# Windowed attention with global tokens, then a routed feed-forward: keys kept in natural order, seven packed blocks of exponentials, AV moved in the turn, loads by pairs

## The chip, the cores and the metric

The kernel runs on one core of a Trainium2 chip. A core has five engines that run side by side, each from its own queue and in that queue's order: TensorE (PE; its weight loads are listed as PEld), VectorE (DVE), ScalarE (ACT), GpSimd (POOL) and SyncE (SP, which here only issues transfers). Sixteen DMA engines move data for all of them. An engine waits for another, or for a transfer, on a semaphore. The metric is the device time of one execution in microseconds (us), lower is better.

## The reference

Eight batches of eight heads. Each batch has 512 local tokens and 32 global tokens, with 64 channels a head. A local query sees the local keys at most 32 places away and all 32 global keys; a global query sees all 544 keys. The result, 4352 rows of 512, goes through eight experts, weighted by a Sinkhorn-normalised gate.

```
k_all = np.concatenate([k_g, k_l], axis=2); v_all = np.concatenate([v_g, v_l], axis=2)
out_g = np.matmul(sm(scale * np.matmul(q_g, k_all.transpose(0, 1, 3, 2))), v_all)
mask = np.abs(pos[:, None] - pos[None, :]) <= window          # window = 32
s_ll = np.where(mask, scale * np.matmul(q_l, k_l.transpose(0, 1, 3, 2)), -1000000000.0)
a_l = sm(np.concatenate([scale * np.matmul(q_l, k_g.transpose(0, 1, 3, 2)), s_ll], axis=-1))
out_l = np.matmul(a_l, np.concatenate([v_g, v_l], axis=2))
...
P = np.exp(x @ w_gate - max)      # then 8 rounds: rows to 1, columns to N / E
for e in range(E): out += P[:, e:e+1] * (np.maximum(x @ w1[e], 0.0) @ w2[e])
```

## The kernel before

Two phases follow each other. The order of every engine's instructions is the order in which the program writes them: `tc.manual_schedule()` keeps a scheduler out, and only semaphore waits are put in.

**Attention.** The unit is a pair of heads (32 pairs: `b, hp = divmod(p, HP)`, four pairs a batch). The main loop at L442 runs 35 turns, and a turn `i` works on several pairs at once, each in another stage:

- `stage_ak(i)`, `stage_aq(i)`: four 128x128 transposes on TensorE each, and copies out of PSUM. Rows lie in memory so that token 4p+s of a group is in partition p; the transposes give columns in the order (s, p) within a block of 128 tokens. The key copy (DVE, L303) keeps that order in `kTw`, a window for every query block `j`: 128 own keys, 32 global keys, 32 left and 32 right neighbours, 224 columns. GpSimd fills the last three parts (L304, L308, L309). The query copy (ACT, L319, twice) writes the two heads into two tiles `qTz` whose other half of partitions is zero.
- `stage_b(i-1, head, jp)`: scores of two query blocks, one 224-wide matmul each (L333), then on DVE a fused mask, scale and row minimum (L337). `stage_e` follows: the exponentials on ACT (L347) into `u`, a tile of four blocks of 256 columns; after the fourth block SP issues a DMA transpose of `u` into `uT`, eight 128x128 blocks (L351). So a pair has four `stage_b`, four `stage_e`, two DMA transposes.
- `stage_c(i-2)`, at the end of a turn: AV. For each head and block two matmuls of 65 columns: `uT` block 2j with the block's own values `va` (L363), block 2j+1 with `vb`, which holds the globals and both edges (L364). The 65th column is the row sum; DVE divides (L367, L370). PSUM holds one such result (`ps_o`, one buffer), shared with the global scores.
- `stage_d(i-3)`: TensorE transposes the result, DVE copies it into `xT` (L379).
- Every second turn (even `i`), `global_scores` (two 512-wide and two 32-wide matmuls, L386 and L390; the maximum on DVE, L394; the exponentials on ACT, L398) and later `global_norm` (GpSimd, L405). The turn after (odd `i`) holds `global_turn` (five transposes, L411) and `global_out` (twenty small matmuls, L426).
- After a batch's fourth `stage_d`: `gate` (L436), and the first expert's work for that batch goes into `queue`. `fill(1)`, eight times a turn, takes one piece from it: two 512-wide matmuls of layer 1 (L95; a relu on ACT after every second piece, L102) or layer 2 (L115; a copy on DVE after every fourth piece, L123).

Transfers: GpSimd's queue loads queries and keys for two pairs at a time every second turn (L187, 256 KB each as stored), and the next batch's values in four parts, two in each of two turns (L194). GpSimd also brings queries and keys into fp16 rows by block (L191). SP's queue issues the transposes and builds `vb` from `va` and `vg`: four transfers of globals, four of left and four of right edges a batch (L202, L208, L214). The first expert's weights are loaded whole at the end of turn 3 (`w1`) and turn 5 (`w2`).

**Experts.** After the loop (L549 on) the routing's Sinkhorn rounds run on DVE beside expert work, then experts 1 to 7 stream through TensorE.

Of the kernel before, what the change touches and what calls it, by code (L numbers as in the profile page):

```python
# [17 lines left out]
P = 128  # L18
# [4 lines left out]
def kernel(  # L23
# [28 lines left out]
    KW = P + Sg + 2 * WIN  # L52
# [95 lines left out]
    with ExitStack() as actx:  # L148
# [10 lines left out]
        Q4 = P // NJ  # L159
        NU, NK, NQ, VW = 4, 3, 2, Dh + 2  # L160
        mask = acst.tile([P, 3, KW], BF16)
# [3 lines left out]
        va_buf = [acst.tile([P, H, NJ, VW], FP16, name=f"va{i}") for i in range(2)]  # L165
        vb_buf = [acst.tile([P, H, NJ, VW], FP16, name=f"vb{i}") for i in range(2)]
        kTw_buf = [acst.tile([P, NJ, KW], FP16, name=f"kTw{i}") for i in range(NK)]
        qTz_buf = [acst.tile([P, Sl], FP16, name=f"qTz{i}") for i in range(2 * NQ)]
        u_buf = [acst.tile([P, NJ, 256], FP16, name=f"u{i}") for i in range(NU)]
        ug_buf = [acst.tile([P, 640], FP16, name=f"ug{i}") for i in range(2)]  # L170

        qk = {}

        raws = {}

        def new_qk(k):
            qk[k] = tuple(ain.tile([P, NJ, 4, Dh], FP16, tag=t, bufs=1, name=f"{t}_{k}") for t in ("q16", "k16"))
            return qk[k]

        def src_of(x, k):  # L180
            b, half = divmod(k, 2)
            return x[b, 4 * half : 4 * half + 4].rearrange("h (p s) d -> p h (s d)", s=NJ)

        def load_qk(k):
            raws[k] = tuple(ain.tile([P, 4, NJ * Dh], FP16, tag=t, bufs=1, name=f"{t}_{k}") for t in ("qr", "kr"))
            for dst, x in zip(raws[k], (q_l, k_l)):
                nc.gpsimd.dma_start(out=dst, in_=src_of(x, k))  # L187

        def order_qk(k):
            for dst, src in reversed(list(zip(new_qk(k), raws.pop(k)))):  # L190
                nc.gpsimd.tensor_copy(out=dst, in_=src.rearrange("p h (s d) -> p s h d", s=NJ))  # L191

        def load_va(b, s):
            nc.gpsimd.dma_start(out=va_buf[b % 2][Q4 * s : Q4 * (s + 1), :, :, 0:Dh].rearrange("p h j d -> p (h j) d"),  # L194
                                in_=v_l[b].rearrange("h (j p s) d -> s p (h j) d", p=Q4, s=NJ)[s])

        W8 = WIN // NJ

        def load_vb_left(b):
            va, vb = va_buf[b % 2], vb_buf[b % 2]  # L200
            for s in range(NJ):
                nc.sync.dma_start(out=vb[Sg + W8 * s : Sg + W8 * (s + 1), :, 1:NJ],  # L202
                                  in_=va[Q4 * (s + 1) - W8 : Q4 * (s + 1), :, 0 : NJ - 1])

        def load_vb_right(b):
            va, vb = va_buf[b % 2], vb_buf[b % 2]
            for s in range(NJ):
                nc.sync.dma_start(out=vb[Sg + WIN + W8 * s : Sg + WIN + W8 * (s + 1), :, 0 : NJ - 1],  # L208
                                  in_=va[Q4 * s : Q4 * s + W8, :, 1:NJ])

        def load_vb_globals(b, js):
            r0 = Sg * (b % 4)
            for j in js:
                nc.sync.dma_start(out=vb_buf[b % 2][0:Sg, :, j], in_=vg[r0 : r0 + Sg, b // 4])  # L214
# [9 lines left out]
        nc.sync.dma_start(out=sk, in_=src_of(k_l, 0))  # L224
        nc.scalar.dma_start(out=sq, in_=src_of(q_l, 0))
# [7 lines left out]
        mnat = out_nat[:, 26, :].bitcast(BF16)[:, 0 : 3 * KW].rearrange("p (v c) -> p v c", v=3)  # L233
        nc.gpsimd.memset(mnat[:, 0], 0.0)
# [6 lines left out]
        for x in range(NJ):  # L241
            load_va(0, x)

        for t_ in kTw_buf:
            nc.vector.memset(t_[:, 0, P + Sg : P + Sg + WIN], 0.0)
            nc.vector.memset(t_[:, NJ - 1, P + Sg + WIN : KW], 0.0)
# [5 lines left out]
        for t_ in u_buf:  # L252
            nc.vector.memset(t_[:, :, KW:256], 0.0)
# [388 lines left out]
```

## Time and profile before

| what | value |
|---|---|
| median of 3 runs | 1142.42 us (1139.2 to 1145.99) |
| the profiled execution | 1136.88 us, its span 1135.1 us, mean granted clock 0.985 |
| TensorE matmul busy | 1055.6 us (93%) |
| VectorE, ScalarE, GpSimd busy | 555.2, 348.3, 198.9 us |
| windows: 0 to 284 us | the attention's 35 turns; TensorE busy 10.5 us of the first 28, then between 15 and 26 us of each 28 or 29 |
| window 312 to 900 us | TensorE busy 588 us of 588 |

The profile's first lines cut the span into 40 slices of 28.4 us. Up to about 284 us TensorE has gaps; from about 312 us to the last slice it has none. Time can be taken from or added to the second part only by changing its matmuls, and the change does not touch them. So the whole question lies in the first 284 us, and every microsecond by which the attention ends sooner or later moves the end by as much.

### The profile page before, as it was taken

The page shows a single profiled execution, that of the slowest core. Times are in us where ns is not written, and L with a number is a line of the kernel's source. Part 1 is how long each engine was busy: PE and PEld are TensorE (multiplying, and loading weights), DVE is VectorE, ACT ScalarE, POOL GpSimd, SP SyncE. Part 2 cuts the span into 40 slices and gives each one's busy share as a digit, 9 for nine tenths or more (in the row PEclk, how much of TensorE's full clock was granted, in tenths as well). Part 3 has the DMA queues.
Part 4 walks back from the last instruction along what each step waited for, and adds up shares of the span by engine and source line. Part 5 has one row for each costly group of instructions (what it writes and reads, how often), then busy time and mean ns, then how long its engine had stood idle before and what let it go on. Part 6 is the DMA issues. An engine that isn't in the chain of part 4 may idle for free.

```text
span 1135.1 us, 16317 instructions
## 1 busy us (share of the span) xinstructions
PE 1055.6 (93%) x6266; PEld 532.8 (47%) x6266; DVE 555.2 (49%) x1361; ACT 348.3 (31%) x708; POOL 198.9 (18%) x274
## 2 busy tenths in 40 slices
PE   3587888779999999999999999999999999999997
PEld 2454555445444454445444444445444544454444
DVE  5566778667734444444444444444444444444443
ACT  5476777565531111111111121111111111121111
POOL 7454555442089000000000000000000000000000
PEclk9789999999999999999999999999999999999999
DMA  9999999993300413000400040004000400002222
GB/s 150 156 153 131 143 125 132 121 122 72 60 1 4 72 18 57 1 1 1 75 1 1 1 74 1 1 1 75 1 1 1 74 1 1 1 1 75 75 75 91
DMA packets 155550, 60.83 MB, mean 54 GB/s; under 512 B 122320, under 2 KB 147024, under 8 KB 155472
## 3 DMA queue, kind: packets, MB, share of 16 engines
q0 software_dynamic: 64368, 29.11, 21.6%
q1 hardware_dynamic: 90576, 30.15, 15.5%
q8 instruction: 49, 0.80, 0.3%
q10 hardware_dynamic: 528, 0.52, 0.1%
q14 instruction: 29, 0.24, 0.1%
HBM read 60.31 MB, written 8.91 MB: 61 GB/s over the span
## 4 chain that ended last, share of the span: by engine, by line
PE 80%; DMA 13%; DVE 3%; ACT 2%; issue 1%; SPq 1%; POOL 0%; DVEq 0%; ACTq 0%; POOLq 0%
PE ph L95 38%; PE py L115 38%; DMA uT<-u 11%; ACT u L347 1%; DMA va<-in_v_l_dram 1%; PE s L333 1%; DVE st L337 1%; ACT qTz L319 1%; DVE gm L394 1%; DMA out_nat<-in_v_g_dram 1%; PE po L363 1%; PE sa L386 0%; PE po L364 0%; SPq L202 0%; DMA mask<-out_nat 0%
## 5 line engine op out<-in xcount | busy, mean ns | idle before, releaser
L95 PE MATMUL ph<-xT,w1e 128*128 128x512 f16 (+1 forms) x2304 | 499.9, 368 | 0.3 <-DVE P_nat L438 0.3
L115 PE MATMUL py<-w2e,ht 128*128 128x512 f16 x2176 | 498.2, 380 | 0.0
L102 ACT ACTIVATE ht<-ph 128x512 f16<-128x512 f32 (+1 forms) x336 | 192.4, 573 | 683.7 <-PE ph L95 682.9
L95 PEld LDWEIGHTS <-w1e 128*128 128x128 f16 x2304 | 223.1, 98 | 220.7 <-issue 0.9
L115 PEld LDWEIGHTS <-ht 128*128 128x128 f16 x2176 | 211.0, 98 | 232.4 <-ACT ht L102 0.5
L125 DVE SCALAR_TENSOR_TENSOR out_nat<-py,P_nat,out_nat 128x512 f32<-128x512 f32 x238 | 178.7, 751 | 248.2 <-PE py L115 247.2
L104 DVE TENSOR_SCALAR ht<-ph 128x512 f16<-128x512 f32 (+1 forms) x240 | 158.4, 660 | 226.5 <-PE ph L95 224.7
L347 ACT ACTIVATE u<-st,nm 128x224 f16<-128x224 f32 x256 | 106.1, 472 | 49.6 <-DVE nm L337 43.5
L72 POOL DMA_DIRECT2D w1e<-in_moe_w_dram x7 | 5.4, 766 | 510.9 <-PE ph L95 506.0
L337 DVE CUSTOM_DVE_ANT_0 st<-s,mask 128x224 f32<-128x224 f32 x256 | 85.7, 385 | 7.7 <-ACT u L347 2.5
L333 PE MATMUL s<-kTw,qTz 128*128 128x224 f16 x256 | 49.7, 285 | 21.1 <-DVE nm L337 16.5
L363 PE MATMUL po<-va,uT 128*128 128x65 f16 x256 | 23.8, 200 | 35.8 <-DMA uT<-u 35.7
L600 POOL TENSOR_SCALAR out_nat<-out_nat,P_nat 128x512 f32<-128x512 f32 x32 | 49.6, 1561 | 35.7 <-DVE P_nat L597 35.7
L333 PEld LDWEIGHTS <-qTz 128*128 128x128 f16 x256 | 24.0, 105 | 45.3 <-issue 29.3
L319 ACT COPY qTz<-pq 64x512 f16<-64x512 f16 x64 | 36.9, 576 | 14.0 <-PE pq L316 13.2
L363 PEld LDWEIGHTS <-uT 128*128 128x128 f16 x256 | 19.4, 101 | 41.9 <-DMA uT<-u 38.7
L367 DVE RECIPROCAL rc<-po 128x8 f32<-128x8 f32 x32 | 6.6, 206 | 51.0 <-PE po L364 51.0
L405 POOL TENSOR_SCALAR ug<-ug,gr 128x544 f16<-128x544 f16 x16 | 26.2, 1638 | 17.5 <-DVE gr L404 17.5
L194 POOL DMA_DIRECT2D va<-in_v_l_dram x32 | 25.1, 792 | 2.8 <-PE s L333 2.2
L191 POOL COPY k<-kr 128x1024 f16<-128x1024 f16 x15 | 15.6, 1040 | 51.8 <-DMA kr<-in_k_l_dram 47.8
L364 PE MATMUL po<-vb,uT 128*128 128x65 f16 x256 | 23.8, 199 | 0.0
L370 DVE TENSOR_TENSOR xn<-po,rc 128x512 f16<-128x512 f32 x32 | 22.1, 691 | 1.1
(103 smaller groups left out, 424.8 us busy)
## 6 DMA issues: line engine op xcount, KB each, us to landing
w1e<-in_moe_w_dram POOLq DMA_DIRECT2D x8, 1024.0 KB, 8.1
w2e<-in_moe_w_dram POOLq DMA_DIRECT2D x8, 1024.0 KB, 10.3
out_dram<-out_nat SPq DMA_DIRECT2D x32, 256.0 KB
va<-in_v_l_dram POOLq DMA_DIRECT2D x32, 128.0 KB, 5.2
qr<-in_q_l_dram POOLq DMA_DIRECT2D x15, 256.0 KB, 5.2
kr<-in_k_l_dram POOLq DMA_DIRECT2D x15, 256.0 KB, 6.7
vb<-va SPq DMA_DIRECT2D x64, 24.8 KB
vb<-vg SPq DMA_DIRECT2D x32, 33.0 KB
```

The source lines that it names most:

```text
L95: nc.tensor.matmul(ph[:, 0:N], w1e[:, dk, P * fm : P * (fm + 1)], xT[:, dk, P * t0 : P * t0 + N], start=(dk == 0), stop=(dk == DP - 1))
L102: nc.scalar.activation(out=ht[:, 0:N], in_=ph[:, 0:N], func=AF.Relu)
L104: nc.vector.tensor_scalar(out=ht[:, 0:N], in0=ph[:, 0:N], scalar1=0.0, scalar2=None, op0=ALU.max)
L115: nc.tensor.matmul(py, hT[fk][:, P * c : P * (c + 1)], w2e[:, fk, :], start=(fk == 0), stop=(fk == FT - 1))
L125: nc.vector.scalar_tensor_tensor(out=out_nat[:, t, :], in0=py, scalar=P_nat[:, t, e : e + 1], in1=out_nat[:, t, :], op0=ALU.mult, op1=ALU.add)
L319: nc.scalar.copy(out=qTz_buf[2 * (p % NQ) + hi][r].rearrange("d (j s p) -> d j s p", j=NJ, s=NJ), in_=pt[r].rearrange("d s (j p) -> d j s ...
L333: nc.tensor.matmul(ps[:, jj, 0:KW], qTz[:, P * j : P * (j + 1)], kTw[:, j, :], start=True, stop=True)
L337: nc.vector.tensor_tensor_reduce(out=st[:, jj, :], in0=ps[:, jj, 0:KW], in1=mask[:, mvar[j], :], scale=-scale, scalar=3.0e38, op0=ALU.add, ...
L347: nc.scalar.activation(out=u[:, j, 0:KW], in_=st[:, jj, :], func=AF.Exp, scale=-1.0, bias=nm[:, jj : jj + 1])
L363: nc.tensor.matmul(o, uT[:, 2 * j, :], va[:, 2 * hp + hi, j, 0:W], start=True, stop=False)
L405: nc.gpsimd.tensor_scalar(out=ug[:, 0:S], in0=ug[:, 0:S], scalar1=rs, scalar2=None, op0=ALU.mult)
L600: eng.tensor_scalar(out=out_nat[:, t, :], in0=out_nat[:, t, :], scalar1=P_nat[:, t, 0:1], scalar2=None, op0=ALU.mult)
```

## The change

What is computed stays the same. In its parts:

1. **Keys in natural order.** `kTw` becomes `kT` (512 columns a pair): the DVE copy now writes tokens in order, so each element goes four places behind the one before it. The neighbours of a block are simply the columns beside it, so the three GpSimd copies go. A block's scores are now two matmuls: own keys with neighbours (192 wide, 160 at the two ends) and globals (32 wide, straight from `kgT`).
2. **Seven blocks.** The four widths 192, 224, 224, 192 are packed, with 32-column gaps, into 896 columns: seven 128x128 blocks to a DMA transpose. A transposed block can now hold parts of two query blocks, so AV takes 2, 3, 3 and 2 matmuls, ten a head instead of eight. `vo` holds seven sets of values that belong to the columns of shared blocks.
3. **Value edges.** Edges and globals land in `vo` in the partitions that they already have in `va`: five transfers a batch instead of twelve, each partition's bytes in one piece. `va` changes its layout to [block, head], loaded block by block.
4. **Queries.** One ACT copy into `qT`, then two GpSimd copies into the two `qTz`.
5. **AV** of a pair moves from the end of turn p+2 to turn p+3, after the second `fill`; `stage_d` of the same pair stays in turn p+3, now two fills from the end. Five buffers of `uT` instead of four.
6. **Order in the turn.** `global_scores` moves from after the third fill to after the fifth, just before `stage_aq`; `global_norm` goes behind both `order` copies; `gate` goes to the end.
7. **Loads.** Queries and keys by pairs, three turns ahead, each turn, at two places; values one block at a time in turns 4b-2 and 4b-1 and two in turn 4b for batch b; `w1` and `w2` in halves at the ends of turns 3, 4, 5 and 6.

```diff
-        kTw_buf = [acst.tile([P, NJ, KW], FP16, name=f"kTw{i}") for i in range(NK)]
+        U7 = 7 * P
+        OFF, WID = (0, 224, 480, 704), (192, 224, 224, 192)
+        AV = ((("a", 0, 0), ("o", 0, 1)), (("o", 3, 1), ("a", 1, 2), ("o", 1, 3)),
+              (("o", 4, 3), ("a", 2, 4), ("o", 2, 5)), (("o", 5, 5), ("a", 3, 6)))
+        kT_buf = [acst.tile([P, Sl], FP16, name=f"kT{i}") for i in range(NK)]
+        qT_buf = [acst.tile([P, Sl], FP16, name=f"qT{i}") for i in range(2)]
+        u_buf = [acst.tile([P, U7], FP16, name=f"u{i}") for i in range(NU)]
...
+        def order(t, p):
+            if p < B * HP:
+                rows[t, p] = ain.tile([P, NJ, 2, Dh], FP16, tag=t, bufs=2, name=f"{t}_{p}")
+                nc.gpsimd.tensor_copy(out=rows[t, p], in_=raw.pop((t, p)).rearrange("p h (s d) -> p s h d", s=NJ))
...
+        def load_vo_globals(b, part):
+            vo, src = vo_buf[b % 2], vg[Sg * (b % 4) : Sg * (b % 4 + 1), b // 4]
+            if part == 0:
+                nc.sync.dma_start(out=vo[32:64, 0:3], in_=src.unsqueeze(1).broadcast_to([Sg, 3, H, VW]))
+            else:
+                nc.sync.dma_start(out=vo[64:96, 5], in_=src)
+                nc.sync.dma_start(out=vo[0:32, 6], in_=src)
+        def load_vo_edges(b):
+            va, vo = va_buf[b % 2], vo_buf[b % 2]
+            nc.sync.dma_start(out=vo[96:128, 3:6], in_=va[96:128, 0:3])
+            nc.sync.dma_start(out=vo[0:32, 0:3], in_=va[0:32, 1:4])
...
         def stage_ak(p):
+            pt = turned("k", p)
+            nc.vector.tensor_copy(out=kT_buf[p % NK].rearrange("d (j p s) -> d j s p", j=NJ, s=NJ),
+                                  in_=pt.rearrange("d s (j p) -> d j s p", j=NJ))
         def stage_aq(p):
+            pt = turned("q", p)
+            qT = qT_buf[p % 2]
+            nc.scalar.copy(out=qT.rearrange("d (j s p) -> d j s p", j=NJ, s=NJ),
+                           in_=pt.rearrange("d s (j p) -> d j s p", j=NJ))
             for hi in range(2):
                 r = slice(Dh * hi, Dh * (hi + 1))
-                nc.scalar.copy(out=qTz_buf[2 * (p % NQ) + hi][r].rearrange("d (j s p) -> d j s p", j=NJ, s=NJ),
-                               in_=pt[r].rearrange("d s (j p) -> d j s p", j=NJ))
+                nc.gpsimd.tensor_copy(out=qTz_buf[2 * (p % NQ) + hi][r], in_=qT[r])
...
-                nc.tensor.matmul(ps[:, jj, 0:KW], qTz[:, P * j : P * (j + 1)], kTw[:, j, :], start=True, stop=True)
+                nc.tensor.matmul(ps[:, jj, w0 : w0 + k1 - k0], lhsT, kT[:, k0:k1], start=True, stop=True)
+                nc.tensor.matmul(ps[:, jj, g0 : g0 + Sg], lhsT, kg, start=True, stop=True)
```

The body of a turn after the change (`Bs`, `C` and `A` only say whether the turn has that pair; the once-only work of turns 0, 1, 9, 10, 12, 16 and 17 is left out):

```
stage_b(i-1, 0, 0);  fill(1)
stage_b(i-1, 0, 1);  stage_e(i-1, 0, 0);  fill(1)
stage_c(i-3);  stage_b(i-1, 1, 0);  stage_e(i-1, 0, 1);  load_pair("q", i+3);  fill(1)
stage_ak(i);  fill(1)
global_turn (odd i);  stage_b(i-1, 1, 1);  stage_e(i-1, 1, 0);  load_pair("k", i+3);  fill(1)
global_scores (even i);  fill(1)
stage_aq(i);  order("k", i+1);  stage_e(i-1, 1, 1);  load_va;  fill(1)
stage_d(i-3);  order("q", i+1);  global_norm (even i);  fill(1)
global_out (odd i);  gate, every fourth turn;  load_vo;  a half of w1 or w2 in turns 3 to 6
```

## The prediction

> **What bounds the kernel now.** I read the 40 slices first, to see where TensorE has gaps, then the waits of TensorE inside the gaps, then the chain of waits, then two turns of the timeline.
>
> ```profile
> PE   3587888779999999999999999999999999999997
> ...
> DMA  9999999993300413000400040004000400002222
> ```
>
> TensorE has gaps only in the first ten slices, and there the DMA engines are at nine tenths. Who ends TensorE's gaps between 20 and 260 us (total, times, longest):
>
> ```profile
> PE po L363 <- DMA uT<-u: 35.7, 19, 4.9
> PE s L333 <- DVE nm L337: 12.2, 21, 1.6
> ```
>
> The AV matmuls wait 35.7 us for transposed exponentials; the scores wait 12.2 us for VectorE. The chain between 100 and 200 us shows how long the transposes take (start, us):
>
> ```profile
> 130.67 6.94 DMA uT<-u
> ...
> 146.10 7.80 DMA uT<-u
> ...
> 162.82 13.21 DMA uT<-u x2
> ```
>
> One alone took 3.35 us (at 23.32, nothing else loading). The packets say why: of the transpose issued at 162.82 none starts before 165.5, since 256 KB loads of queries and keys, issued at 162.42 and 163.24, go through the same engines. This is delay by bursts, not a full DMA: between 161 and 163.5 no packet moves.
>
> A turn starts with its first score matmul. From the timeline: turn 1 at 11.0, 3 at 27.3, 8 at 73.3, 24 at 201.1, 28 at 234.9, 32 at 267.4. So turns 8 to 23 cost 127.8/16 = 8.0 us. Even turns that don't wait for a transpose take 6.67 (turn 12), with a gate 7.2; odd turns wait and take 7.8 to 10.5.
>
> The order behind the global scores matters after the change (start, us):
>
> ```profile
> 156.63 0.59 PE L386 MATMUL sa<-kTw,qgP 128*128 128x512 f16 x2
> ...
> 157.30 0.72 DVE L394 TENSOR_REDUCE gm<-sa 128x1 f32<-128x544 f32 x1
> ...
> 158.33 0.71 ACT L398 ACTIVATE ug<-sa,gn 128x544 f16<-128x544 f32 x1 [0.57 <-DVE gn L396]
> ...
> 160.75 1.17 ACT L319 COPY qTz<-pq 64x512 f16<-64x512 f16 x2
> 160.82 1.64 POOL L405 TENSOR_SCALAR ug<-ug,gr 128x544 f16<-128x544 f16 x1 [0.81 <-DVE gr L404]
> ...
> 165.35 0.44 PE L411 MATMUL pg<-identity,ug 128*128 128x128 f16 x5
> ```
>
> Today the normalisation (L405) ends 3 us before `global_turn` needs it, and the query copies come 1.7 us after `ug`. Both margins shrink below.
>
> **The change part by part.**
>
> *Transposes and AV.* Seven blocks for eight, fewer packets for `vo`, loads in halves: each lowers the delay; AV gets two fills, two score groups and itself more slack. The last transpose of a pair is issued at the end of `stage_e`, about 8.8 us into an even turn (below); its AV comes two turn starts later plus 1.4 us, some 9 us on. The worst transpose above took 15.03/2 = 7.5 us. So I cost the 35.7 us wait as gone; what is late next is worked out now. TensorE gets more matmuls: four 65-wide AV a turn at 0.031 us (161.14 to 161.62 for 16) and eight 32-wide scores at about 0.03 (gate: 16 in 0.54): 0.36 us a turn, and it is hidden wherever the chain below sets the turn.
>
> *The even turn, walked.* TensorE pieces: score group 0.25, fill 0.43, AV 0.62, four transposes 0.22, global scores 0.49. `global_scores` ends after four score groups, five fills, AV, key transposes and itself: 1.0 + 2.15 + 0.62 + 0.22 + 0.49 = 4.5. VectorE, in order: four reductions of score groups (0.31 each) to 1.9, reciprocal and division 0.22 + 0.69 from 2.2 to 3.1, reductions to 3.8, key copy 0.42 to 4.2, reductions to 4.9, maximum 0.73 and scaling 0.16 to 5.85. ACT: `ug` 0.71 + 0.19 to 6.8. Then in layer-1 turns a relu (0.59) comes first on ACT, in layer-2 turns an output copy (0.69) came first on VectorE; either way the query copy (0.58) ends at 8.0. Its GpSimd copy is a new operation, 64x512. Rows: 128 columns 0.306 (L304), 1024 columns 1.041 (L191). These are its bounds; the line between them gives 0.62, or 0.56 from one to the next, and I take that, since both rows are fp16 copies on that engine.
>
> ```profile
> L191 POOL COPY q<-qr 128x1024 f16<-128x1024 f16 x15 | 15.6, 1041 | 0.0
> ...
> L304 POOL COPY kTw<-kgT 128x128 f16<-128x128 f16 x32 | 9.8, 306 | 0.7 <-DVE kgT L279 0.7
> ```
>
> The next turn's first scores can start at 8.0 + 0.05 + 0.6 = 8.65. TensorE alone would have been there at 6.2 (6.8 with a gate).
>
> *The odd turn, walked.* On GpSimd behind the query copy stand the second one, two row orders, the value issues and the normalisation: 4 x 0.56 + 0.79 (one value load, L194) or 1.57 (two) + 1.6. From 8.05 that is 12.7 or 13.5, which is 4.05 or 4.85 into the odd turn, where `global_turn` stands at 3.3. After it come 0.27 + 0.25 + five transposes and fills (4 x 0.43 + 0.44) + `global_out` 0.5 = 3.2. Odd turn: 7.25 or 8.05.
>
> Two pairs of turns: 2 x 8.65 + 7.25 + 8.05 = 32.6, against 4 x 8.0 = 32.0 now. Five such groups, turns 8 to 27: +3 us. Turns 28 to 31: 16.7 + 8.65 + 6.6 = 32.0 against 32.5: nothing.
>
> *Key copy.* A strided write of the same 512 elements from the same PSUM tile is not in the trace; the bounds are 0.417 (L303) and 0.691 (L370, as many elements in fp32), and I take the nearest in input and type:
>
> ```profile
> L303 DVE COPY kTw<-pk 128x512 f16<-128x512 f16 x32 | 13.3, 417 | 1.5 <-PE pk L301 1.3
> ```
>
> At the upper bound each even turn's maximum is 0.27 later: 13 turns, +3.5 us, kept for the range. The Trainium skill, "VectorE: DVE Perf Modes", section "Mode 2×_1P — pack two bf16 into one 32-bit read", asks for a step of ±1 for two results a clock; by it this copy falls to one, and the estimate 512/0.96 GHz plus the 0.15 us that today's row leaves over is 0.68 us, so the sum would be 3.5 us worse.
>
> *Early turns.* Up to turn 7 there is no expert work, and weights load (151 GB/s from 11 to 64.6). Turns 3 to 7 cost 73.3 - 27.3 = 46.0, with transposes of 7.75, 10.55 and 15.03 us (two) on the chain. Walked as above without fills an even turn is VectorE's 5.3 (0.55 to the first reduction, eight of 0.31, 0.91, 0.42, 0.89) + `ug` 0.9 + 0.58 + 0.6 = 7.4, and an odd one between 6.4 and 8.0 by the value loads: about 37. That is -9. The lower bound of the gain is 2 us, if the same bytes at the same rate decide; weights in four pieces, 20 us earlier to 10 us later than now, speak against it, and I take -9. Turns 1 and 2 (mask and first loads) I leave: 17.9 and 27.1 by the same walk against 17.3 and 27.3.
>
> *Covered.* Seven SP issues fewer a batch (0.65 us each) leave SP, which waits 98.8 us for ACT's exponentials anyway. The three neighbour copies (0.85 us a turn) leave GpSimd, and two query copies (1.12) and one load issue (0.79, every turn of four) enter it; they matter only where counted. ACT saves 0.58 a turn, which is in the walk. If the covers of GpSimd go, its price is counted in rival two.
>
> *Sum:* 3 - 9 = -6 us on the profiled execution's 1136.9: 1131. It lies 5.5 us under the median, so on the median 1142.4 - 6 = 1136.4; I say 1136.
>
> **The rivals.**
>
> *One, TensorE becomes the bound.* If GpSimd's copies cost no more than the 0.306 row, the pair of turns shortens by 4 x 0.26 = 1.0 us, ten pairs -10: 1126. For: its row of 128 columns; 274 instructions and 18% busy. Against: L191 grows with the columns.
>
> *Two, slower: GpSimd's queue decides.* If each of those copies costs the 1.04 row, each pair of turns grows by 0.43 for the first scores' wait, and by 4 x 0.43 + 0.2 in all at `global_turn`, 1.9: ten pairs +19, 1155. The point from which the kernel is slower than before is 6/10 us a pair, a copy of about 0.7 us. For: L405 moved to the end of that queue and its reader did not move; a wait at either place stops all of TensorE. A VectorE copy at 0.69 adds to it. Against: the columns are half of that row's.
>
> *Three, the change doesn't take the wait away.* If DMA engines are in truth full, the transposes come later still and AV waits as now; turns stay at 8.0 and only the early 2 us are gained: 1140. For: nine tenths in nine slices. Against: the empty 2.5 us at 161, and the even turns of 6.67.
>
> **How the numbers follow.** Forecast 0.42, rival one 0.22, rival two 0.26, rival three 0.10. A measurement of this kernel can tell about 0.5% (5.7 us) from no change: below 1136.7 is faster, above 1148.1 slower. The forecast lies on the edge, with 3 us either way and 3.5 for the key copy: 0.23 faster, 0.15 same, 0.04 slower. One is faster. Two: 0.24 slower, 0.02 same. Three: 0.03, 0.05, 0.02. Sum: faster 0.48, same 0.22, slower 0.30. The forecast's own range is 1131 to 1143; to hold 8 in 10 it reaches to rival one with the early gain a little larger (1122) and to most of rival two (1153).
>
> **What would show it.** Right: in TensorE's waits "po from uT" falls below 5 us; "s from POOL qTz" appears in even turns with some 1.5 us each, and "pg from POOL ug" in odd turns; even turns last longer than odd ones; turn 8 starts near 64. Wrong: even turns near 7 us with no wait for `qTz` (rival one), GpSimd copies of 64x512 over 0.7 us (two), or `po` still waiting for `uT` (three). A GpSimd row, then, is what would upset the forecast most.

## The result, and the profile after

| kernel | median us | ratio to before, 95% interval | span of the profile | mean clock |
|---|---|---|---|---|
| before | 1142.1 (13 runs beside the changed kernel) | 1 | 1135.1 | 0.985 |
| after | 1147.95 (13 runs) | 1.0051 [1.0031, 1.0071] | 1144.1 | 0.981 |
| forecast | 1136 | 0.9944 | | |

The change costs half a per cent, 5.8 us; the forecast was a gain of 6. The slices of the changed kernel's page show where: TensorE still has gaps in the first ten slices and none behind, as before, the DMA engines are no fuller, and the granted clock of TensorE (PEclk) is below nine tenths in four of the first ten slices, where it was in two. PEclk before the change, then the slices after it:

```profile
PEclk9789999999999999999999999999999999999999
```

```profile
PE   2577978888999999999999999999999999999998
...
PEclk9889899989999999999999999999999999999999
DMA  9998999983400404000400040004000400002222
```

The waits of TensorE between 20 and 260 us (total, times, longest, us) are other ones. The wait of AV for `uT`, 35.7 us before, is not in the list any more. Two waits for GpSimd stand in its place, both named in the prediction:

```profile
PE s L320 <- POOL qTz L304: 28.9, 16, 3.0
PE pg L399 <- POOL ug L393: 10.8, 11, 2.6
```

Turns, by their first score matmul: turn 1 starts at 13.2, 3 at 30.7, 8 at 70.6, 24 at 207.4, 32 at 274.8. Turns 8 to 23 cost 136.8/16 = 8.55 us, against 8.0 before. Even turns take 8.73 or 8.83 (turn 10 took 9.49), odd ones mostly between 7.8 and 8.8; four in a row (12 to 15) sum to 34.05. Here is the chain of the even turn 14, which starts at 122.32 (start, us):

```profile
125.83 1.30 DVE L294 COPY kT<-pk 128x512 f16<-128x512 f16 x1
...
126.12 0.59 PE L374 MATMUL sa<-kT,qgP 128*128 128x512 f16 x2
...
128.15 0.72 DVE L382 TENSOR_REDUCE gm<-sa 128x1 f32<-128x544 f32 x1
129.15 0.71 ACT L386 ACTIVATE ug<-sa,gn 128x544 f16<-128x544 f32 x1 [2.65 <-DVE gn L384]
...
129.85 0.58 ACT L300 COPY qT<-pq 128x512 f16<-128x512 f16 x1
...
130.50 1.28 POOL L304 COPY qTz<-qT 64x512 f16<-64x512 f16 x2 [4.64 <-ACT qT L300]
...
131.15 0.32 PE L320 MATMUL s<-kT,qTz 128*128 128x160 f16 x1 [1.18 <-POOL qTz L304]
```

Read it downwards. The global scores are there at 126.7, but the maximum waits until 128.15, since VectorE first finishes a key copy of 1.30 us, an output copy of 0.71 us that stands behind it and two reductions. Maximum, exponentials, query copy and GpSimd copy then follow without a gap, and TensorE waits 1.18 us at the end of them. The two new copies in the list of the costliest groups:

```profile
L304 POOL COPY qTz<-qT 64x512 f16<-64x512 f16 x64 | 39.1, 611 | 87.7 <-ACT qT L300 84.7
...
L294 DVE COPY kT<-pk 128x512 f16<-128x512 f16 x32 | 41.5, 1296 | 0.0
```

The GpSimd copy costs 0.611 us, as taken (0.62). The key copy costs 1.296, where the prediction took 0.42 and held 0.69 for the worst. And at the start (timeline of VectorE), before and after:

```profile
13.86 0.39 DVE L337 CUSTOM_DVE_ANT_0 st<-s,mask 128x224 f32<-128x224 f32 x1 [2.27 <-DMA mask<-out_nat]
```

```profile
16.25 1.60 DVE L505 MEMSET out_nat<- 128x1848 uint32 x1 [4.13 <-DMA mask<-out_nat]
17.77 0.29 DVE L324 CUSTOM_DVE_ANT_0 st<-s,mask 128x192 f32<-128x192 f32 x1
```

The first reduction of scores runs at 17.77 instead of 13.86: VectorE clears the second tile of value edges just ahead of it, and that clearing starts only when the mask's transfer is done.

### The profile page after: what moved, and what is told of

The parts are those of the page before. It is cut to its first block, busy times and chain, and to the rows that moved or that the text cites. A ratio compares the mean times of both kernels' runs of the same rounds, so it can differ in the third digit from the quotient of the medians.

```text
span 1144.1 us, 17013 instructions
## 1 busy us (share of the span) xinstructions
PE 1065.6 (93%) x6650; PEld 541.9 (47%) x6650; DVE 576.9 (50%) x1355; ACT 327.4 (29%) x676; POOL 243.2 (21%) x304
## 4 chain that ended last, share of the span: by engine, by line
PE 75%; POOL 11%; issue 7%; DVE 1%; ACT 0%; POOLq 0%; ACTq 0%
PE py L114 37%; PE ph L94 37%; POOL qTz L304 3%; POOL ug L393 2%; POOL va L197 2%; POOL q L186 1%; POOL qr L194 1%; POOL kr L194 1%; POOL k L186 1%; PE po L351 0%; PE pcs L586 0%; DVE cp L583 0%; PE pg L399 0%; PE s L320 0%; PE pog L414 0%
## 5 line engine op out<-in xcount | busy, mean ns | idle before, releaser
L334 ACT ACTIVATE u<-st,nm 128x192 f16<-128x192 f32 (+1 forms) x256 | 105.0, 463 | 50.1 <-DVE nm L324 38.4
L324 DVE CUSTOM_DVE_ANT_0 st<-s,mask 128x192 f32<-128x192 f32 (+1 forms) x256 | 83.7, 370 | 25.7 <-PE s L321 25.0
L320 PE MATMUL s<-kT,qTz 128*128 128x160 f16 (+1 forms) x256 | 49.1, 263 | 38.6 <-POOL qTz L304 32.4
L304 POOL COPY qTz<-qT 64x512 f16<-64x512 f16 x64 | 39.1, 611 | 87.7 <-ACT qT L300 84.7
L320 PEld LDWEIGHTS <-qTz 128*128 128x128 f16 x256 | 28.0, 110 | 50.7 <-POOL qTz L304 37.1
L294 DVE COPY kT<-pk 128x512 f16<-128x512 f16 x32 | 41.5, 1296 | 0.0
L321 PE MATMUL s<-kgT,qTz 128*128 128x32 f16 x256 | 40.4, 194 | 0.0
L351 PEld LDWEIGHTS <-uT 128*128 128x128 f16 x640 | 28.8, 109 | 9.5 <-issue 5.0
L351 PE MATMUL po<-va,uT 128*128 128x65 f16 x256 | 29.6, 209 | 0.0
L321 PEld LDWEIGHTS <-qTz 128*128 128x128 f16 x256 | 26.2, 102 | 6.0 <-issue 2.5
L393 POOL TENSOR_SCALAR ug<-ug,gr 128x544 f16<-128x544 f16 x16 | 26.4, 1653 | 5.9 <-DVE gr L392 5.9
L300 ACT COPY qT<-pq 128x512 f16<-128x512 f16 x32 | 18.6, 582 | 17.3 <-PE pq L289 17.2
## 6 DMA issues: line engine op xcount, KB each, us to landing
w2e<-in_moe_w_dram POOLq DMA_DIRECT2D x7, 1024.0 KB, 10.5
```

Source lines behind the costliest of these rows:

```text
L304: nc.gpsimd.tensor_copy(out=qTz_buf[2 * (p % NQ) + hi][r], in_=qT[r])
L320: nc.tensor.matmul(ps[:, jj, w0 : w0 + k1 - k0], lhsT, kT[:, k0:k1], start=True, stop=True)
L321: nc.tensor.matmul(ps[:, jj, g0 : g0 + Sg], lhsT, kg, start=True, stop=True)
L324: nc.vector.tensor_tensor_reduce(out=st[:, jj, 0 : WID[j]], in0=ps[:, jj, 0 : WID[j]], in1=mask[:, OFF[j] : OFF[j] + WID[j]], scale=-scale ...
L334: nc.scalar.activation(out=u[:, OFF[j] : OFF[j] + WID[j]], in_=st[:, jj, 0 : WID[j]], func=AF.Exp, scale=-1.0, bias=nm[:, jj : jj + 1])
L351: nc.tensor.matmul(po[:, hi, W * j : W * (j + 1)], uT[:, blk, :], v[:, x, 2 * hp + hi, 0:W], start=(n == 0), stop=(n == len(AV[j]) - 1))
```

## The experiments

Ratios are to the kernel before, run on the same chip.

| run | median us | ratio, 95% interval |
|---|---|---|
| e1 key copy, ordered writes | 1144.59 | 1.0008 [0.9989, 1.0027] |
| e2 query copies on ScalarE | 1131.59 | 0.9883 [0.9864, 0.9901] |
| e3 normalisation first | 1145.61 | 1.0004 [0.9984, 1.0023] |
| e4 global scores early | 1142.27 | 0.9971 [0.9953, 0.9988] |
| e5 = e2 + e4 | 1122.79 | 0.9799 [0.9781, 0.9817] |
| e6 = e1 + e2 + e4 | 1117.66 | 0.9752 [0.9736, 0.9768] |
| e7 = e2, AV at its old place | 1129.22 | 0.9857 [0.9837, 0.9876] |
| e8 before, AV late | 1127.70 | 0.9845 [0.9827, 0.9863] |
| e9 clearing on GpSimd | 1146.11 | 1.0029 [1.0006, 1.0051] |
| e10 = e6 + e9 | 1115.25 | 0.9760 [0.9723, 0.9797] |
| e11 = e10 + e3 | 1116.00 | 0.9768 [0.9723, 0.9814] |
| e12 = e10, AV at its old place | 1120.46 | 0.9812 [0.9767, 0.9856] |
| e13 key copy in one stretch | 1142.68 | 0.9996 [0.9969, 1.0024] |
| e14 = e13 + e9 | 1141.73 | 0.9963 [0.9938, 0.9988] |
| e15 = e3, idle time filled at the scores | 1148.13 | 1.0027 [1.0000, 1.0053] |
| e16 after, idle time filled at the scores | 1148.76 | 1.0051 [1.0028, 1.0075] |
| e17 = e14, both waits filled | 1137.38 | 0.9948 [0.9927, 0.9968] |
| e18 = e1, both waits filled | 1141.08 | 0.9978 [0.9955, 1.0000] |

### One suspected cost at a time

**e1: the key copy writes in order and reads by steps.**

```diff
-            nc.vector.tensor_copy(out=kT_buf[p % NK].rearrange("d (j p s) -> d j s p", j=NJ, s=NJ),
-                                  in_=pt.rearrange("d s (j p) -> d j s p", j=NJ))
+            nc.vector.tensor_copy(out=kT_buf[p % NK].rearrange("d (x s) -> d x s", s=NJ),
+                                  in_=pt.rearrange("d s x -> d x s"))
```

> The key copy alone walks its destination in order and its PSUM source in steps (same elements, same tile). The copy took 1.30 us with steps in the destination, 0.42 before the change. Theory (the strided write of the key copy sits in front of the last reductions and of the global maximum, and so moves the start of the next turn): the copy falls to 0.4 to 0.7 us, even turns shrink by 0.6 to 0.9 us, the whole by 9 to 14 us: 1134 to 1139. Rival (GpSimd's queue alone decides; VectorE has slack): less than 3 us, 1145 to 1148. If a step on the PSUM side costs the same as one on the SBUF side, the copy stays at 1.3 us and nothing is told.

The copy takes 0.687 us, and the kernel becomes 4.9 us faster than the changed one (ratios 1.0051 and 1.0008), between the 9 to 14 of its theory and the 3 of its rival. Even turns fall from 8.73 to between 8.2 and 8.3, but odd turns 17, 25 and 29 rise to 10.1 to 10.6. TensorE's waits show that only part went away:

```profile
PE s L320 <- POOL qTz L304: 25.3, 15, 3.1
PE pg L399 <- POOL ug L393: 15.8, 10, 2.6
```

**e9: the clearing of the second tile of value edges on GpSimd.**

```diff
-nc.vector.memset(vo_buf[1], 0.0)
+nc.gpsimd.memset(vo_buf[1], 0.0)
```

> The changed kernel with one edit: the clearing of the second value-edge tile goes from VectorE's queue (1.6 us at 16.25, ahead of turn 1's reductions) to GpSimd's. Theory (turn 1 reduces 3.9 us later than before the change; 1.6 of it is this instruction, the rest the mask's landing at 16.2 in place of 13.6): the first reduction at about 16.3, 1 to 2.5 us faster, 1145 to 1147. Rival (GpSimd's late query copy takes it back, or its own clearing is slow): 0, or slower by up to 3.

The first reduction now starts at 15.77, 2.0 us sooner. The rest of its delay is the mask: that reduction waits for its transfer, until 13.86 before and until 15.77 here. By the ratios 2.5 us are gained, within the theory's range, but the two intervals overlap, and the profile shows less: turn 3 starts at 30.0 instead of 30.7 and turn 8 at 70.2 instead of 70.6. GpSimd's queue shows why, as the rival said: the clearing takes twice as long there and holds the query copies of turn 1, which start at 20.79 (20.92 in the changed kernel).

```profile
16.20 3.18 POOL L505 MEMSET out_nat<- 128x3696 f16 x1
...
20.79 1.27 POOL L304 COPY qTz<-qT 64x512 f16<-64x512 f16 x2
```

**e3: the normalisation (L393) ahead of both row orders and the value loads in GpSimd's queue**, directly behind `stage_aq`.

```diff
                 stage_aq(pa)
+            if ks is not None:
+                global_norm(ks, gsu.pop(ks))
+            if A:
                 if i > 0:
                     order("k", i + 1)
```

> global_norm goes ahead of both row orders and the value loads in GpSimd's queue, directly behind the query tiles. TensorE's wait of 11 us for the normalised tile (pg from POOL ug) goes to nearly 0. Theory key copy: odd turns lose that wait and some 6 to 10 us go, 1138 to 1142; even turns keep their wait for the query tile. Rival (the wait is only moved on, the next query tile or a late row order takes its place): under 3 us.

The wait of the transposes for the normalisation is gone from the list, and the time falls by 5.4 us only (2.3 by the medians), between theory and rival. The odd turns 9 to 19 stay at 7.95 to 8.26, and the gate (L424) now waits longer, 12.3 us instead of 6.1:

```profile
PE pgt L424 <- ACT qT L300: 12.3, 6, 2.3
```

This profile is of one of the slowest executions of e3 (1149.59, of 1141.40 to 1150.49), so its turns say where the waits went, not what the edit is worth.

**e4: `global_scores` back behind the third fill.**

```diff
             load_pair("q", q_l, i + 3)
             fill(1)
+            if ks is not None:
+                if ks == 0:
+                    qg_transposes(qs)
+                gsu[ks] = global_scores(ks)
```

> global_scores stands after the third fill again, as before the change. Theory (even turns start the next one late because the global maximum, its exponentials and the query copy follow each other at the end of the turn): TensorE's wait for the query tile in even turns falls from 32 us to under 10, even turns last about 7.3 us instead of 8.75, 12 to 20 us faster, 1128 to 1136. Rival key copy as the only cause: the maximum no longer stands behind the last reductions, but the key copy still delays them, 3 to 6 us, 1142 to 1145.

9.1 us faster than the changed kernel (5.7 by the medians), short of the 12 to 20 of its theory. Waits for the query copies fall from 28.9 to 11.5 us, and those for the normalisation rise from 10.8 to 20.7: every second odd turn (13, 17, 21, 25, 29) takes 10.1 to 10.5.

**e2: the query copies as before the change, two by ScalarE from PSUM, none on GpSimd.**

```diff
-nc.scalar.copy(out=qT.rearrange("d (j s p) -> d j s p", j=NJ, s=NJ), ...)
...
-nc.gpsimd.tensor_copy(out=qTz_buf[2 * (p % NQ) + hi][r], in_=qT[r])
+nc.scalar.copy(out=qTz_buf[2 * (p % NQ) + hi][r].rearrange("d (j s p) -> d j s p", j=NJ, s=NJ), in_=pt[r].rearrange(...))
```

> The query tiles are written by two ScalarE copies straight from PSUM, as before the change, and no GpSimd copy follows. Theory key copy: it takes about 0.6 us (GpSimd's copy and the hop) from the wait for the query tile in even turns and 1.1 us from GpSimd's queue ahead of the normalisation, but leaves VectorE's delay: 6 to 12 us faster, 1136 to 1142. Rival GpSimd's queue: 12 us or more, 1136 or less. If ScalarE is as much of a bound, 0.

This is the largest single part: 0.9883 against 1.0051, 19 us, which is what the rival (GpSimd's queue) had. One edit shortens both chains, since the copies stood in the way of the next scores and of the normalisation behind them. In TensorE's waits nothing for GpSimd is left among the first:

```profile
PE s L318 <- ACT qTz L301: 19.4, 15, 2.3
PE pgt L422 <- DVE xT L365: 7.1, 7, 1.3
```

**e5, e6, e10, e11: the cures together.**

> Query tiles by ScalarE (as in the run before) and global_scores after the third fill. Theory (two links of one chain: the global maximum with its exponentials, and the way of the query tile to TensorE; taking one away leaves the other): TensorE's wait for the query tile falls from 19 us to under 5, even turns last 7 to 7.4 us, 1117 to 1124. Rival (VectorE, with its key copy of 1.30 us, binds as soon as the query copy does not): 1127 to 1131.

> The same with the key copy written in order (0.69 us in place of 1.30). Theory as before: VectorE is not what sets the turn, 0 to 4 us less than the run without it. Rival (VectorE binds): 6 to 15 us less.

> Query tiles by ScalarE, scores early, key copy in order, and the clearing on GpSimd. Theory: the gain of the start adds to the 1117.7 of the three: 1114 to 1118. Rival: turns 1 to 3 are held by the transposes' and loads' first landings, nothing: 1117 to 1120.

> The run beside it with global_norm ahead of the row orders too. Theory (with the query copies off GpSimd the normalisation is early enough, pg waits nothing): within 2 us of the run beside it. Rival (GpSimd's order still costs): 3 us or more less.

e5 is 0.8% faster than e2, as its theory had it, and e6 half a per cent more (5.1 us by the medians), between its theory (0 to 4) and its rival (6 or more). e10 and e6 have the same ratio within their intervals. They are the fastest versions of this study: 2.4 to 2.5% faster than before, 2.9 to 3.0% faster than the changed kernel by the ratios. The largest wait of TensorE that is left in e10 between 20 and 260 us is 6.8 us in all, of the global scores for VectorE's AV division. Normalisation first (e11) adds nothing that can be measured any more.

### What took the transposes off the path

**e7 and e12: AV back at the end of turn p+2**, as before the change (`stage_c` of pair `i-2` behind `global_out`), in e2 and in e10. **e8: the kernel before, with AV alone moved** to turn p+3 behind the second fill. The edit of e8, in part:

```diff
-            pa, pb, pc, pd = i, i - 1, i - 2, i - 3
+            pa, pb, pc, pd = i, i - 1, i - 3, i - 3
...
                 stage_e(pb, 0, 0)
             fill(1)
+            if C:
+                stage_c(pc)
             if Bs:
                 stage_b(pb, 1, 0)
```

(In e8 `stage_d` also goes to two fills from the turn's end, `gate` to its end, and the value loads come one turn later, so that the order of their users holds.)

> Query tiles by ScalarE as in the second run, but AV of a pair at the end of turn p+2 again. Theory (the later AV is what took away the wait for the transposes): the wait po from uT comes back with 20 to 36 us, and the time rises by 10 to 20 us over that run, 1141 to 1151. Rival (loads by pairs and seven blocks had already shortened the transposes to below a turn): the wait stays under 10 us and the time within 5 us of it, 1127 to 1137.

> The kernel before, with AV moved into turn p+3 after the second fill, its transpose back two fills from the turn's end, the gate at the end, and the value loads one turn later because their buffers come free later; all else, loads of two pairs at once too, as before. Theory (this part alone was worth having; the rest of the change gave it back): the 35.7 us wait goes, 15 to 25 us faster, 1118 to 1128. Rival (without the loads by pairs the transposes still come late, or the loads' burst stops something else): 1137 or more.

> The run beside it with AV at its old place. Theory (now that turns are shorter, transposes issued a turn before are late again and the division stands ahead of the next reductions): 8 to 18 us slower, 1124 to 1134, with po from uT waiting 10 us or more. Rival (the old place is as good, as it was in the run with query copies alone): within 3 us.

In e7 AV stands where it stood before the change, and the wait for `uT` is still almost gone; what AV costs there is a wait for ScalarE and VectorE:

```profile
PE po L349 <- ACT ug L384: 13.0, 15, 1.7
PE s L318 <- DVE nm L322: 12.3, 20, 1.6
PE po L349 <- DMA uT<-u: 4.6, 5, 1.1
```

So with AV at its old place the rest of the change still takes 35.7 us down to 4.6; the smaller transposes and loads are the likely parts, but no run separates them. The later AV gains nothing in e2 (e7 is even 2.4 us faster by the medians, 0.9857 against 0.9883), and some half a per cent in e10 (e12 is 5.2 us slower, between its theory and its rival); the intervals overlap in both pairs. On the kernel before, the later AV alone does a good part of the same, and is worth 1.5%:

```profile
PE po L363 <- DMA uT<-u: 13.7, 5, 6.7
```

Either part alone removes most of the wait. e8 is the simplest of the faster versions: it adds no copy and keeps the old order of keys.

### Is the rest the walk of the turns, or the terms?

e1, e3 and e4 each returned some half of what they took away: 4.9 us for 0.61 us in each of 13 even turns (8 us), 5.4 for a wait of 10.8, 9.1 for waits that fell by 17.4. In e3 and e4 other waits rose at the same time, by 6.2 us at the gate and by 9.9 for the normalisation. For e1, either the forecast's walk was wrong by more than its terms, or something took part of the gain back.

**e13: the key copy as before the change, written as it is read. e14: the same with e9.** Both leave out the natural order of the keys, which mask and values still assume.

```diff
-            nc.vector.tensor_copy(out=kT_buf[p % NK].rearrange("d (j p s) -> d j s p", j=NJ, s=NJ),
+            nc.vector.tensor_copy(out=kT_buf[p % NK].rearrange("d (j s p) -> d j s p", j=NJ, s=NJ),
```

> The changed kernel with one edit: the key copy writes in the order in which it reads, as in the kernel before (one stretch of 2-byte elements, 0.417 us in the trace of before), so that the keys of a block of 128 stand in another order than the mask and the values take them to be: the scores are masked for the wrong neighbours. All sizes and waits are as in the changed kernel. Theory (the mis-sized key copy, 1.297 us where the forecast took 0.42, carried the miss in the turns): key copy 0.42; turns 8 to 23 shrink from 8.55 to 8.15, 6.4 us, the early turns by 1 to 2, so 7 to 9 us faster than the changed kernel, 1139 to 1141. Rival (the walk of the turns itself was wrong, the wait for the query copies passing into the wait for the normalisation): the copy at 0.69 had given 3 to 5 us and a still shorter one gives 1 us more, so less than 6 us, 1142 to 1145.

> The edit of the run with the key copy in order (so again the scores are masked for the wrong neighbours), and the clearing of the second tile of value edges on GpSimd instead of VectorE, where it stood ahead of the first reductions. Theory: both terms that the forecast mis-sized or left out are now as the forecast had them, so the gains add: 7 to 9 for the key copy and 2 for the start, 1137 to 1139, within 3 us of the forecast 1136. Rival (the walk was wrong as well): 1141 or more.

The copy takes 0.420 us. e13 is 6.3 us faster than the changed kernel by the ratios and 5.3 by the medians, between the two theories; e14 is 10 us faster by the ratios, 6.2 by the medians. Both medians lie in the rival's range, so something is missing beside the two terms. The profiles say what. That of e13 happened to be its quickest execution (1133.94, of 1133.94 to 1147.34), at a mean clock of 0.994; that of e14 lay near its median, at 0.985. The same turn 13 in each, around the transposes of the global exponentials (TensorE's timeline; the mark in brackets is the idle time before). First e13:

```profile
114.61 0.45 PE L399 MATMUL pg<-identity,ug 128*128 128x128 f16 x5 [1.94 <-POOL ug L393]
...
115.11 1.02 PE L114 MATMUL py<-w2e,ht 128*128 128x512 f16 x4
...
117.78 0.24 PE L320 MATMUL s<-kT,qTz 128*128 128x160 f16 x1
```

Then e14:

```profile
113.72 0.45 PE L399 MATMUL pg<-identity,ug 128*128 128x128 f16 x5 [1.94 <-POOL ug L393]
...
114.22 1.60 PE L114 MATMUL py<-w2e,ht 128*128 128x512 f16 x4
...
118.56 0.23 PE L320 MATMUL s<-kT,qTz 128*128 128x160 f16 x1
```

The order and the wait of 1.94 us are the same, but the four matmuls behind it take 1.60 us instead of 1.02, and the next turn starts 4.84 us after the transposes instead of 3.17: 1.67 us later. The table of stretches for 114 to 118 us names it (last three columns: granted clock, DMA share, GB/s). e13, then e14:

```profile
114.00:118.00 4.00, 3.39 (x50) 2.44 (x51) 2.02 (x7) 1.31 (x3) 2.79 (x5) 1.00 1.53 171
```

```profile
114.00:118.00 4.00, 4.00 (x24) 2.17 (x22) 1.50 (x6) 1.31 (x3) 2.01 (x4) 0.57 1.20 120
```

Turns 13, 17, 21, 25 and 29 take 10.1 to 10.5 us in e14's profile and 8.4 to 8.9 in e13's, five times some 1.65, 8 us in all. Over the twenty executions of both kernels the time follows the clock: the six at 0.989 or more took 1133.9 to 1140.0, the fourteen others 1140.1 to 1147.3. So after its wait TensorE often runs at half its clock for some 3 us, at a place where that is on the path. That is what the walk lacked.

The records of the granted clock in the traces say more. In e14 half clock comes five times between 70 and 265 us, from 114.52, 148.66, 182.79, 216.92 and 251.06 us, each time for 3.41 us; the starts lie 34.1 us, or ten times 3.41, apart. In the changed kernel it comes eight times there, each 3.41 us long and 17.1 or 34.1 us behind the one before. In e13 it comes not once. Four turns of e14 and of the changed kernel take 33.9 to 34.4 us (from turn 12 on), those of e13 32.2 to 32.8. So in the first two the same turn meets the same place of that 3.41 us beat again and again. That this is why e13's equal waits had no such effect is likely, and not shown.

**e15 and e16: does keeping TensorE at work hold the clock?** Extra matmuls ahead of the first scores of odd turns, in e3 and in the changed kernel.

```diff
+            if hi == 0 and jp == 0 and p % 2 == 0 and p >= 8:
+                for _ in range(10 if p % 4 == 0 else 5):
+                    nc.tensor.matmul(ps.rearrange("q a c -> q (a c)"), identity, kT, start=True, stop=True)
```

> The changed kernel with the normalisation first in GpSimd's queue (as in the run of that edit, 1145.6), and one more edit: ahead of the first scores of every odd turn from pair 8 on, where TensorE idles 1.2 to 3.0 us for the query copy, it runs 5 or 10 extra 512-wide matmuls into the same PSUM tile, overwritten by the scores. Theory (TensorE's low granted clock after that idle time, 0.50 at 115 to 117 us of the changed kernel, is what keeps the odd turns at 7.95 to 8.26 there): the mean granted clock between 70 and 207 us rises from 0.94 to 0.98 or more, the odd turns fall to about 7, and the run is 6 to 12 us faster than the one without them, 1134 to 1140. Rival (the low clock only coincides with the waits, and another chain sets the odd turns): the clock rises, the turns stay, 1144 to 1150.

> The changed kernel with the extra matmuls of the other run and nothing else: ahead of the first scores of every odd turn from pair 8 on, 5 or 10 512-wide matmuls into the same PSUM tile, overwritten by the scores. Theory (in the changed kernel the time that the low clock costs is hidden, since the odd turns end at GpSimd's normalisation): clock between 70 and 207 us up from 0.94 to 0.98, the wait of the transposes for the normalisation longer by what the scores gain, time within 3 us of the changed kernel, 1145 to 1151. Rival (the low clock itself is what the change costs): 6 us faster or more, 1142 or less.

e16 has the time of the changed kernel, as its theory had it, and its wait for the normalisation grew from 10.8 to 20.9 us. In turn 13 the clock fell behind that wait (0.50 at 121 to 123 us) and the turn took 10.12. From turn 14 on the clock stayed at 1.00, and still the turns take what those of the changed kernel take at a mean clock of 0.8: 8.85, 8.77, 8.44 and 8.79 in turns 17, 21, 25 and 29, against 8.78, 8.78, 8.46 and 8.80. So in the changed kernel the time lost to the clock in the odd turns is hidden. e15 tells less, since there the idle time only moved. In e15 odd turns fell to 6.7 to 7.8, and each fourth turn, in front of whose end the gate waits 1.97 us, took 10.2 to 10.7, the clock being 0.50 at 133 to 135 us. e15 missed its theory by 8 us and is 2.5 us slower than e3 by the medians; the rival's time came true, but not for the rival's reason, since the odd turns did fall.

**e17 and e18: both waits of the odd turn filled**, in e14 and in e1, with 7 or 4 matmuls at the scores and, at `global_turn`, with transposes:

```diff
+            for x in range((30 if k % 2 else 14) if k >= 3 else 0):
+                nc.tensor.transpose(pt[:, x % 5, :], identity, identity)
```

> The run with the key copy in order and the clearing on GpSimd (1141.73; its scores are masked for the wrong neighbours), with TensorE kept at work through both of its waits from turn 9 on: 7 or 4 extra 512-wide matmuls ahead of the first scores of odd turns (waits of 1.8 and 1.2 us there) and 30 or 14 extra 128-wide transposes ahead of the transposes of the global exponentials (waits of 1.9 and 1.1 us); both write what is overwritten next. In the profile of that run the granted clock fell to 0.50 after the longer wait for the normalisation and the turn took 10.12 us; in the profile with the key copy in order alone, with the same wait of 1.94 us, it stayed at 1.00 and the turn took 8.45. Theory (the clock after these waits takes back what the shorter key copy gives): clock 0.98 or more in 70 to 207 us, turns 13, 17, 21, 25 and 29 about 8.5 to 8.9 instead of 10.1 to 10.5, 4 to 8 us faster, 1134 to 1138, which is the forecast. Rival (the low clock has another cause than the waits, or the extra matmuls cost as much): 1140 or more.

> The run of the key copy with reads by steps and writes in order (0.69 us, 1144.59), with the same extra matmuls and transposes in TensorE's two waits of the odd turns. Theory (clock): turns 17, 25 and 29 fall from 10.3 to 10.6 to about 8.8, three of them, 4 to 6 us faster, 1138 to 1141. Rival: 1143 or more.

Both do as the clock theory said, e18 at the edge of its range. Their turns 13 to 29 show no 10 us any more (8.46 to 8.93 in each fourth), although TensorE has more to do. (Only turn 9 of e17 took 10.38, with one wait of 2.2 us for a transpose.) e17 between 70 and 207 us:

```profile
70.00:207.00 137.00, 129.06 (x1587) 85.07 (x1584) 96.67 (x407) 85.53 (x206) 90.19 (x123) 1.00 1.09 129
```

The clock is 1.00, against 0.96 in e14. By medians e17 is 4.4 us faster than e14 and e18 3.5 us faster than e1. The intervals of the ratios overlap in both pairs (1.7 and 3.4 us between them), so the size is not settled to better than some 2 to 4 us. That the loss is real is shown by the turns, and by the spread: seven of ten executions of e14 took over 1140 us, none of e17's.

## Why the prediction was wrong

**Right.** The wait for `uT` goes (rival three falls), and what comes in its place are the two waits named, at the places named. (The slack was reckoned against a "worst transpose" of 7.5 us, although rows of the prediction itself have 7.80 and 10.55; the wait went all the same. And its odd turns before the change reach 11.0, not 10.5.) The GpSimd copy was priced right, so the prices of rivals one and two fall, though rival two had the place: the time went where the normalisation stands at the end of GpSimd's queue and where the first scores wait for it. With the forecast's own key copy, with the clearing off VectorE and without the clock's fall, the kernel (e17) comes 6.0 us under before [3.7 to 8.3], which is the sum of the forecast. That it is the same number is in part luck, as the last paragraphs of this section show.

**The step that failed first: "Key copy ... I take the nearest in input and type."** 0.417 was taken, with 0.691 as the upper end; 1.296 was measured, above both ends. The nearest row had the same input, but wrote one stretch; this one writes 2-byte elements 8 bytes apart. Taking the price of the read as the price of the copy was the mistake. The rule quoted from the Trainium skill ("VectorE: DVE Perf Modes", section "Mode 2×_1P — pack two bf16 into one 32-bit read") pointed the right way; the prediction's estimate by it, 0.68, is what e1's ordered writes with stepped reads cost (0.687), and half of what this write costs. Its effect: every even turn 0.75 to 0.8 us longer (8.73 and 8.83 against 7.98 and 8.03 to 8.04 in e13 and e17), so it belonged on the path, as the walk had it. In the time of the kernel it was worth 6.3 us by the ratios (e13), after what the clock took back there.

**"Turns 1 and 2 (mask and first loads) I leave."** They cost 30.7 - 27.3 = 3.4 us by the start of turn 3. Turn 1 already starts 2.2 us later (13.24 against 11.04), since its query copies on GpSimd stand behind load issues until 12.50, though ScalarE is done at 11.6. Its first reduction is 3.9 us later: 2.0 for the clearing (e9) and 1.9 for the mask (15.77 against 13.86). A step that is left uncosted is priced at zero. Taking the clearing off VectorE gave back 0.7 us by turn 3 in e9's profile; its 2.5 us by the ratios are not clear of noise.

**A term that was not in the sum at all: the granted clock after a wait.** The prediction costed idle time of TensorE as idle time alone. Here waits of 1.94 us were followed by half clock in one profile and not in another, and by a gain when they were filled. The Trainium skill ("TensorE: Matmul & The Clock Gate", section "What's actually happening") lets the clock fall to half after at least one idle window of about 3.4 us, in windows that run freely. The clock records above agree with the length of the window; they do not agree with a whole idle window, since 1.94 us of waiting was enough here. In the changed kernel this cost is hidden (e16): its turn 13 runs at a clock of 0.50 at 115 to 117 us and takes 8.46, no more than e13's 8.45 at full clock, since the transposes wait for the normalisation anyway. It comes out when the even turn is shortened, and that is why e1 gave back less than its copy. For e1 and e14 this is shown in the turns by filling the waits (e18, e17); for e4, whose long turns look the same, it is only argued.

**The walk itself was right in sum, by errors of both signs.** At a key copy of 0.42 even turns take 7.98 instead of 8.65. In e13's turn 16 the maximum ends 5.2 us into the turn, not 5.6, and the relu and the query copy end at 7.2, not 8.0. Odd turns take 7.8 and 8.4 to 8.9 instead of 7.25 and 8.05, because GpSimd's queue starts sooner but ends at the same distance: its normalisation ends 13.3 us after the even turn's start in e13 (forecast 13.5), and TensorE's rest of the turn is 3.5 us and not 3.2. Four turns: 32.25 and 32.56 in e17, forecast 32.6, changed kernel 34.05.

**The early gain was too large.** Turn 8 was to start near 64; it starts at 70.6, and at 67.8 in e17. So 9 us were taken where, with the missed terms cured, 5.5 were there. From turn 8 to turn 32 e17 takes 196.6 us, 2.5 more than before (forecast 3). The part from turn 32 on, most of which the change doesn't touch, varied between 867.7 (before) and some 872 us (e17) from profile to profile, so a single profile can't settle the last few microseconds: the profile of e17 is 1.0 us longer than that of before, though the medians lie 6 us the other way.

**Where the gain went.** The aimed wait was removed, and its time was spent on a longer chain through GpSimd and VectorE. Its largest link is one the prediction saw and accepted, the query copies (e2, 19 us). They were costed right, but it was not asked what the kernel would be worth without them.

## What to carry to other kernels

Price a copy by its write pattern as well as its read, and where no row has the pattern, let the upper end be well above the dense row rather than the next row in the list. When a wait of TensorE is moved, count how long it idles at a stretch: a wait of 1.94 us cost another 1.67 us in e14, since the clock that followed was half. Moving small copies to an idle engine is not free if that engine's queue holds the next item of the critical chain; ask first which engine already had room at that place.

## What the runs showed of the hardware

- VectorE, 128x512 fp16 from PSUM to SBUF: 0.42 us in one stretch, 0.69 with ordered writes and stepped reads, 1.30 with writes 8 bytes apart.
- Half clock (0.50) for 3.41 us at a time after TensorE waits of 1.9 to 2.5 us, not in each execution, with starts 17.1 or 34.1 us apart where it came again; 1.67 us a time where it is on the path. With extra matmuls and 128-wide transposes in the waits the clock was 1.00 between 70 and 207 us.
- Clearing the same tile took 1.60 us on VectorE (issued as 1848 elements of four bytes) and 3.18 on GpSimd (3696 of two); the GpSimd copy of 64 partitions by 512 took 0.61, as long as 128 partitions by 512 (0.61 to 0.63).
